# Attention and two MLPs on one core: each group of score and value matmuls ranked to run as one block on TensorE

## The chip, the cores and the metric

The kernel runs on one core of one Trainium2 chip. The metric is the device time of one execution in microseconds. Three runs of the kernel before took 1076.14 to 1080.6 us, with a median of 1076.39 us. The profile is of one execution, whose span from the first to the last instruction is 1075.8 us.

## The reference

Three layers follow each other. Shapes are those of the inputs.

```python
def _attn_ref(q, k, v, f):            # q, k, v: (4, 8, 576, 64), f: (4, 8, 576)
    scores = scale * np.matmul(q, k.transpose(0, 1, 3, 2))
    cum = np.cumsum(np.log(np.clip(f, 0.0001, 1.0)), axis=-1)
    scores = np.where(causal, -1000000000.0, scores + cum[:, :, :, None] - cum[:, :, None, :])
    attn = np.exp(scores - np.max(scores, axis=-1, keepdims=True))
    attn = attn / (np.sum(attn, axis=-1, keepdims=True) + 1e-09)
    return np.matmul(attn, v)
# x = attention's output as 2304 tokens of 512
# MLP 1: h = x @ w_in; r = max(h, 0); x = (s * r * r + b) @ w_out     (512 -> 2048 -> 512)
# MLP 2: h = x @ w_in; g = max(0.01 * h, h); out = g @ w_out          (512 -> 2048 -> 512)
```

## The kernel before

**Units.** The queries of each of the four batches are cut into a first unit (256 queries) and a second one (320 queries: two blocks of 128 and a tail of 64). A unit's eight heads are worked off in pairs. Attention on unit u+1 runs while MLP 1 works on unit u, so that TensorE (PE) gets two kinds of work in one stream. When attention is over, the rest of MLP 1 and then MLP 2 run alone.

**Attention's matmuls.** `mm_score` makes one score group for the two heads of a pair: for each query block two float32 matmuls with 64 rows, one for each head, on the lower and upper half of the partitions (L290), and then bfloat16 matmuls of an identity with a mask (L300). The 64 tail queries of both heads are one tile of two float32 matmuls with 128 rows (L279) and one mask matmul (L282). All go to one PSUM tile `ps_s`, of which there is one buffer. `st_score` reads it with VectorE (L320) and ScalarE takes the exponential (L338). `st_split` makes float16 high and low parts (L363 on ScalarE, L364 on VectorE) into `p_hl` (three buffers), and a transposing DMA on SyncE's queue brings them to `p_t` (L368, three buffers). `st_av` then issues the value products into `ps_v` (L385): float16, a weight load of 128 columns and a matmul each, with 128 columns for a block of queries and 64 for a tail. A tile of one head has 6 or 8 products, a tail 20 for the two heads; there are 104 such groups.

**The MLP's matmuls.** MLP 1 goes through 16 blocks of 128 hidden columns. `mlp1_h` issues 12 matmuls of 256 columns into `ps_h` (L696) and `mlp1_o` issues 12 of the block before into `ps_o` (L740; L737 in the first unit). Between them `mlp1_g` makes `g` out of `ps_h`: three passes on ScalarE (L718, L719, L720) and one on VectorE (L721). Operands are in the 4-byte format float32r, each value as a high and a low part, hence three products. MLP 2 has the same form in float32r with 512 columns (L798, L814).

**What sets the order.** The program is traced, and a scheduler with its own timeline of each engine then picks, for each engine, the next instruction among those that it holds ready; of several it takes the one with the highest rank. The rank follows the order of the source, shifted by `tc.high_priority(offset=n)`: `slots_to` traces each attention slot with a shift of 150 (scores, splits) or 90 (value products). The result is a fixed order for each engine, and semaphores for what crosses engines. On the chip each engine works its list in that order.

Of the kernel before, what the change touches and what calls it, by code (L numbers as in the profile page):

```python
# [1 line left out]

# [15 lines left out]
P = 128  # L18
UN = 256
# [19 lines left out]
def attention_moe_moe_kernel(  # L39
# [15 lines left out]
    nc = tc.nc  # L55
# [11 lines left out]
    NL = S - 2 * UN  # L67
# [80 lines left out]
    ident_h = const.tile([P, P], BF16, name="ident_h")  # L148
    mask_h = const.tile([P, P], BF16, name="mask_h")
    mask_l = const.tile([P, NL], BF16, name="mask_l")  # L150
# [35 lines left out]
    def q_cols(u):  # L186
        return UN + (2 * NL if units[u][2] > UN else 0)
# [6 lines left out]
    qk_p, cumk, v_raw, v_st, v_inv = {}, {}, {}, {}, {}  # L194
# [41 lines left out]
    def split_v(j, kend):  # L236
# [22 lines left out]
        for r in range(2):  # L259
# [3 lines left out]
                in_=hl[r * D : (r + 1) * D, :nk].rearrange("p k l c -> p (k l c)"),  # L263
            )

    def mm_score(i):

        jb, n, ts, last = tiles[i]
        u, h, j, half = jobs[jb]
        if not half and h % 2:  # L270
            return
        b, u0, un, _ = units[u]
        qk = qk_p[j // 2]
        qn = q_cols(u)
        ps = s_t[i] = ps_a.tile([P, 2, 512], F32, tag="ps_s", name="ps_s", bufs=1)
        if half:
            w = (u0 + un) // 2
            for c in range(2):
                nc.tensor.matmul(  # L279
                    ps[:, c, :w], qk[:, UN:qn], qk[:, qn + c * w : qn + (c + 1) * w], start=True, stop=c == 0  # L280
                )
            nc.tensor.matmul(ps[:, 1, w - NL : w], ident_h, mask_l, start=False, stop=True)  # L282
            return
        s_t[i + 1] = ps
        at = [sum(sum(QT[t]) for t in ts[:r]) for r in range(len(ts) + 1)]
        for r, t in enumerate(ts):
            q0, m = QT[t]
            for e in range(2):
                rows = slice(e * D, (e + 1) * D)
                nc.tensor.matmul(  # L290
                    ps[:, e, at[r] : at[r + 1]],
                    qk[rows, q0 - u0 : q0 - u0 + m],
                    qk[rows, qn : qn + q0 + m],
                    start=(r == 0),
                    stop=False,
                )

        for r, t in enumerate(ts):
            for e in range(2):
                nc.tensor.matmul(  # L300
                    ps[:, e, at[r + 1] - P : at[r + 1]], ident_h, mask_h, start=False, stop=(r == len(ts) - 1)
                )

    def st_score(i):
        jb, n, ts, last = tiles[i]
        u, h, j, half = jobs[jb]
        b, u0, un, _ = units[u]
        mm_score(i)
        ps = s_t.pop(i)
        tt = t_t[i] = ap.tile([P, S], F32, tag="tt", name="tt", bufs=4)  # L310
# [32 lines left out]
    def last_of_pair(jb):  # L343
        u, h, j, half = jobs[jb]
        return half or (h % 2 == 1 and units[u][2] == UN)
# [24 lines left out]
    def st_av(i):  # L370
        jb, n, ts, last = tiles[i]
        u, h, j, half = jobs[jb]
        b, u0, un, _ = units[u]
        if half or (n == 0 and h % 2 == 0):
            av_t[j // 2] = ps_a.tile([P, 512], F32, tag="ps_v", name="ps_v", bufs=2)
        av, pt = av_t[j // 2], p_t.pop(i)
        to = 0
        for t in ts:
            q0, m = QT[t]
            nk = -(-(q0 + m) // P)  # L380
            at = 0 if half else q0 - u0 + h % 2 * UN
            for e in range(P // m):
                for k in range(nk):
                    for l in range(2):
                        nc.tensor.matmul(  # L385
                            av[:, at + e * m : at + (e + 1) * m],
                            v_st[j + e][:, k].rearrange("p l d -> p (l d)"),
                            pt[:, to + l * nk + k, e * m : (e + 1) * m],
                            start=(k == 0 and l == 0),
                            stop=(k == nk - 1 and l == 1),  # L390
                        )
            to += 2 * nk
        if not last:
            return
        pr = h // 2
        if not half and h % 2 == 0:
            x_raw[u] = xp.tile([P, UN + NL], F32, tag="x_raw", name="x_raw", bufs=2)
        xr = x_raw[u]
        at = UN if half else 0
        for e in range(2) if half else [h % 2]:  # L400
            own, oth = slice(e * D, (e + 1) * D), slice((1 - e) * D, (2 - e) * D)
            m = NL if half else UN
            src, o = av[:, e * m : (e + 1) * m], xr[own, at : at + m]
            nc.scalar.copy(o, src[oth])
            nc.vector.tensor_tensor(out=o, in0=src[own], in1=o, op=ALU.add)
        if not last_of_pair(jb):
            return
        if pr == 0:
            xs[u] = xp.tile([P, 2, ND, UN], F32R, tag="x", name="x", bufs=2)
        inv = v_inv[j - j % 2][:, 4:5]  # L410
        with ahead(P_X):
            split_x1(xs[u], pr, xr[:, :UN], inv)
            if un > UN:
                xl = xr[:, UN:]
                nc.gpsimd.tensor_scalar(xl, xl, inv, 0.0, ALU.mult, ALU.add)
                nc.sync.dma_start(out=xld[pr * P : (pr + 1) * P, b * NL : (b + 1) * NL], in_=xl)

    def split_x1(x, d, raw, inv):
        nc.scalar.mul(x[:, 0, d], raw, inv)
        nc.vector.scalar_tensor_tensor(x[:, 1, d], raw, inv, x[:, 0, d].bitcast(F32), ALU.mult, ALU.subtract)  # L420
# [10 lines left out]
            )  # L431

    P_ATT, P_AV, P_G, P_W, P_F, P_X = 150, 90, 0, -100, 0, 100

    def ahead(n):
        return tc.high_priority(offset=n)
# [16 lines left out]
    def slot_d(i):  # L453
        if 0 <= i - LAG < NTL:
            st_av(i - LAG)
# [197 lines left out]
    c = 0  # L653
# [37 lines left out]
    def mlp1_h(u, i):  # L691
        x, (wi, wo) = xs[u], w1.get(i)
        ps = h_bank()[:, :UN]
        for d in range(ND):
            for n, (a, c) in enumerate(((0, 0), (0, 1), (1, 0))):
                nc.tensor.matmul(  # L696
                    ps,
                    wi[:, a, d * P : (d + 1) * P],
                    x[:, c, d],
                    start=(d == 0 and n == 0),  # L700
                    stop=(d == ND - 1 and n == 2),
                )
        return ps
# [128 lines left out]
    for u in range(NU):  # L832
# [9 lines left out]
        for i in range(NF):  # L842
# [12 lines left out]
            ps = mlp1_h(u, i)  # L855
# [99 lines left out]
```

## Time and profile before

| what | value |
|---|---|
| median of three runs | 1076.39 us (1076.14 to 1080.6) |
| profiled execution | span 1075.8 us, 18112 instructions |
| PE busy | 1036.2 us, 96% of the span |
| weight loads (PEld) busy | 877.7 us, 82% |
| VectorE, ScalarE, GpSimd busy | 544.3, 521.9 and 152.0 us |
| value products L385 | 912 matmuls, mean 216 ns each |
| score matmuls L290 | 224 records, mean 515 ns each |

A busy PE is not a PE at its peak: matmuls are pipelined, the end of one is modelled, and the mean durations above overlap. What an instruction costs the stream is the distance from its start to the start of the next, which the timeline shows. A float32 matmul (L290, L279) leaves two records in the trace, a float16, bfloat16 or float32r matmul one. The granted clock is 0.984 of full speed as a mean over the span.

### The profile page before, as it was taken

The numbers are of one execution on the slowest core, as the hardware profiler recorded it, in microseconds if no ns is written. First come the engines' busy times: TensorE is split into PE (matmuls) and PEld (weight loads), VectorE is DVE, ScalarE is ACT, GpSimd is POOL, SyncE is SP. The second block draws the span as 40 slices with busy tenths as digits, with TensorE's granted clock in tenths as the row PEclk, the third lists the DMA queues.
The fourth block names the chain that finished last, engine by engine and source line by source line (L and its number), as shares of the span: only waits on it lengthen the run. The fifth ranks groups of instructions, "written<-read, shape, count | busy, mean of one in ns | idle before, by whom it ended". The sixth has DMA issues, their size and how long they took to land.

```text
span 1075.8 us, 18112 instructions
## 1 busy us (share of the span) xinstructions
PE 1036.2 (96%) x6664; PEld 877.7 (82%) x6664; DVE 544.3 (51%) x1410; ACT 521.9 (49%) x1283; POOL 152.0 (14%) x234
## 2 busy tenths in 40 slices
PE   7888889999999999999999999999999999999998
PEld 4677779888787878878899999777888888888897
DVE  5899874665565765766633178983311311211111
ACT  4676786655565655655654366462222221222222
POOL 4334333010010000000000024451000000000000
PEclk9898889999999999999999999999999999999999
DMA  8499372666767866886822083640200100000010
GB/s 285 151 241 254 90 187 48 139 147 124 164 146 150 193 148 142 191 165 134 152 41 79 1 273 119 193 140 1 79 1 1 59 1 1 4 36 1 1 40 20
DMA packets 184296, 116.68 MB, mean 108 GB/s; under 512 B 137040, under 2 KB 163152, under 8 KB 184208
## 3 DMA queue, kind: packets, MB, share of 16 engines
q1 hardware_dynamic: 184208, 115.53, 43.9%
q8 instruction: 52, 0.85, 0.3%
q14 instruction: 36, 0.29, 0.1%
HBM read 74.00 MB, written 10.04 MB: 78 GB/s over the span
## 4 chain that ended last, share of the span: by engine, by line
PE 40%; issue 5%; DVE 3%; POOL 2%; DMA 1%; ACT 1%; SPq 0%; POOLq 0%; ACTq 0%; DVEq 0%
PE ps_o L814 16%; PE ps_h L798 15%; PE ps_o L740 4%; PE ps_h L696 3%; POOL w L111 2%; DVE wt L103 1%; DMA w_raw<-in_moe_w_out 1%; DVE wt L105 1%; DVE wt L102 1%; DMA p_t<-p_hl 0%; PE ps_v L385 0%; ACT wt L101 0%; PE ps_s L290 0%; DVE g L721 0%; DMA xld<-x_raw 0%
## 5 line engine op out<-in xcount | busy, mean ns | idle before, releaser
L696 PE MATMUL ps_h<-x,w 128*128 128x256 f32 x1728 | 275.4, 298 | 5.0 <-POOL w L111 3.3
L696 PEld LDWEIGHTS ps_h<-x,w 128*128 128x128 f32 x1728 | 238.5, 194 | 14.1 <-issue 6.5
L740 PE MATMUL ps_o<-g,w 128*128 128x256 f32 (+1 forms) x1536 | 245.8, 298 | 4.2 <-ACT g L720 1.5
L740 PEld LDWEIGHTS ps_o<-g,w 128*128 128x128 f32 x1536 | 209.8, 192 | 20.5 <-issue 7.6
L814 PE MATMUL ps_o<-w,g 128*128 128x512 f32 x864 | 216.1, 396 | 1.8 <-DVE g L806 1.8
L798 PE MATMUL ps_h<-x,w 128*128 128x512 f32 (+1 forms) x960 | 213.6, 370 | 0.0
L798 PEld LDWEIGHTS ps_h<-x,w 128*128 128x128 f32 x960 | 169.0, 188 | 34.3
L814 PEld LDWEIGHTS ps_o<-w,g 128*128 128x128 f32 x864 | 160.4, 188 | 41.6 <-DVE g L806 3.6
L806 DVE TENSOR_TENSOR g<-ps_h,g 128x512 fp32r<-128x512 f32 (+1 forms) x80 | 51.0, 637 | 258.3 <-ACT g L805 258.1
L804 ACT ACTIVATE ps_h<-ps_h 128x512 f32<-128x512 f32 (+1 forms) x80 | 43.1, 539 | 250.7 <-PE ps_h L798 250.7
L385 PE MATMUL ps_v<-p_t,v_st 128*128 128x128 f16 (+1 forms) x912 | 117.6, 216 | 10.1 <-DMA p_t<-p_hl 5.3
L364 DVE SCALAR_TENSOR_TENSOR p_hl<-tt,sm,p_hl 128x512 f16<-128x512 f32 (+4 forms) x128 | 80.8, 645 | 58.1 <-ACT p_hl L363 57.3
L363 ACT ACTIVATE p_hl<-tt,sm 128x512 f16<-128x512 f32 (+4 forms) x128 | 73.5, 597 | 54.7 <-DMA p_t<-p_hl 44.9
L718 ACT ACTIVATE ps_h<-ps_h 128x256 f32<-128x256 f32 x128 | 47.1, 368 | 92.0 <-PE ps_h L696 90.4
L111 POOL TENSOR_TENSOR w<-wt,w 128x512 fp32r<-128x512 f32 x48 | 73.9, 1542 | 98.5 <-ACT w L110 95.4
L385 PEld LDWEIGHTS <-v_st 128*128 128x128 f16 x912 | 62.7, 98 | 30.6 <-issue 9.1
L338 ACT ACTIVATE tt<-tt,sm 128x512 f32<-128x512 f32 (+4 forms) x128 | 76.2, 596 | 22.1 <-DVE sm L320 21.2
L721 DVE TENSOR_TENSOR g<-ps_h,g 128x256 fp32r<-128x256 f32 x128 | 53.7, 421 | 64.9 <-ACT g L720 63.8
L320 DVE CUSTOM_DVE_ANT_0 tt<-ps_s,cumk 128x512 f32<-128x512 f32 (+4 forms) x128 | 59.7, 498 | 18.4 <-PE ps_s L300 17.2
L290 PE MATMUL ps_s<-qk_p 64*128 64x512 f32 (+3 forms) x224 | 63.1, 515 | 2.1 <-issue 1.4
L101 ACT ACTIVATE wt<-w_raw 128x512 f32<-128x512 f32 x64 | 42.8, 673 | 30.7 <-POOL w L111 19.2
L720 ACT CAST g<-ps_h 128x256 fp32r<-128x256 f32 x128 | 47.0, 369 | 8.5 <-PE ps_o L740 5.3
(91 smaller groups left out, 877.1 us busy)
## 6 DMA issues: line engine op xcount, KB each, us to landing
w_raw<-in_moe_w_in SPq DMA_DIRECT2D x32, 512.0 KB, 6.0
w_raw<-in_moe_w_out SPq DMA_DIRECT2D x32, 512.0 KB, 6.2
cumk<-cumd SPq DMA_DIRECT2D x32, 256.0 KB, 3.9
qk_p<-in_qk SPq DMA_DIRECT2D x16, 480.0 KB, 4.2
x1d<-x1o SPq DMA_DIRECT2D x36, 128.0 KB, 2.8
cumk<-cumd SPq DMA_DIRECT2D x32, 144.0 KB, 3.2
v_raw<-in_v SPq DMA_DIRECT2D x16, 288.0 KB, 3.2
out<-o SPq DMA_DIRECT2D x18, 256.0 KB, 2.4
```

Of the source, the lines that this page charges most:

```text
L111: nc.gpsimd.tensor_tensor(w[:, 1], x, w[:, 0].bitcast(F32), ALU.subtract)
L290: nc.tensor.matmul(ps[:, e, at[r] : at[r + 1]], qk[rows, q0 - u0 : q0 - u0 + m], qk[rows, qn : qn + q0 + m], start=(r == 0), stop=False,)
L320: nc.vector.tensor_tensor_reduce(tt[:, at + k0 : at + k0 + kw], ps[:, c, :kw] if half else ps[:, h % 2, at : at + w], cumk[jb][:, k0 : k0 ...
L338: nc.scalar.activation(e, e, AF.Exp, bias=sm[:, r : r + 1], scale=-1.0, accum_out=sm[:, 2 + r : 3 + r])
L363: nc.scalar.mul(v[:, 0, :w], e, inv)
L364: nc.vector.scalar_tensor_tensor(v[:, 1, :w], e, inv, v[:, 0, :w], ALU.mult, ALU.subtract)
L385: nc.tensor.matmul(av[:, at + e * m : at + (e + 1) * m], v_st[j + e][:, k].rearrange("p l d -> p (l d)"), pt[:, to + l * nk + k, e * m : ( ...
L696: nc.tensor.matmul(ps, wi[:, a, d * P : (d + 1) * P], x[:, c, d], start=(d == 0 and n == 0), stop=(d == ND - 1 and n == 2),)
L721: nc.vector.tensor_tensor(out=g[:, 1, :UN], in0=ps, in1=g[:, 0, :UN].bitcast(F32), op=ALU.subtract)
L740: nc.tensor.matmul(po[d], wo[:, a, d * P : (d + 1) * P], g[:, c], start=(first and n == 0), stop=(last and n == 2),)
L798: nc.tensor.matmul(ps[:, :n], wi[:, a, d * P : (d + 1) * P], x[:, e, d, :n], start=(d == 0 and k == 0), stop=(d == ND - 1 and k == 2),)
L814: nc.tensor.matmul(po[m], g[:, a, m * P : (m + 1) * P], wo[:, e, :], start=(i == 0 and k == 0), stop=(i == NF - 1 and k == 2),)
```

## The change

A constant P_RUN of 4000 is added, and a helper `run_on(first)` that shifts the rank by it unless `first` is true. Of each score group, each tail's score group and each tile's group of value products, the first matmul keeps its rank and all others get the shift. Nothing else differs: every engine has the same instructions as before, in another order.

```diff
+    def run_on(first):
+        return nullcontext() if first else tc.high_priority(offset=P_RUN)
...
         if half:
             w = (u0 + un) // 2
             for c in range(2):
-                nc.tensor.matmul(
-                    ps[:, c, :w], qk[:, UN:qn], qk[:, qn + c * w : qn + (c + 1) * w], start=True, stop=c == 0
-                )
-            nc.tensor.matmul(ps[:, 1, w - NL : w], ident_h, mask_l, start=False, stop=True)
+                with run_on(c == 0):
+                    nc.tensor.matmul(
+                        ps[:, c, :w], qk[:, UN:qn], qk[:, qn + c * w : qn + (c + 1) * w], start=True, stop=c == 0
+                    )
+            with run_on(False):
+                nc.tensor.matmul(ps[:, 1, w - NL : w], ident_h, mask_l, start=False, stop=True)
             return
...
             for e in range(2):
                 rows = slice(e * D, (e + 1) * D)
-                nc.tensor.matmul(
...
+                with run_on(r == 0 and e == 0):
+                    nc.tensor.matmul(
...
                 for k in range(nk):
                     for l in range(2):
-                        nc.tensor.matmul(
...
+                        with run_on(t == ts[0] and e == k == l == 0):
+                            nc.tensor.matmul(
...
     P_ATT, P_AV, P_G, P_W, P_F, P_X = 150, 90, 0, -100, 0, 100
+    P_RUN = 4000
```

The line numbers of PE's matmuls move with the diff: L279 to L283, L282 to L287, L290 to L296, L300 to L307, L385 to L393, L696 to L705 and L740 to L749. The first place below is a score group of a second unit on PE's list (`ps_s_3725`). In the kernel before, with matmuls of MLP 1 (`ps_h_3260`) and single value products of the tail before it (`ps_v_3494`) between its two halves:

```order
L696 MATMUL ps_h_3260<-x_2323,w_383 128x256 x5
L385 LDWEIGHTS v_st_3044
L385 MATMUL ps_v_3494<-p_t_3436,v_st_3044 128x64
L696 MATMUL ps_h_3260<-x_2323,w_383 128x256
L290 MATMUL ps_s_3725<-qk_p_3397 128x512
L385 LDWEIGHTS v_st_3044
L385 MATMUL ps_v_3494<-p_t_3436,v_st_3044 128x64
L696 MATMUL ps_h_3260<-x_2323,w_383 128x256
L385 LDWEIGHTS v_st_3044
L385 MATMUL ps_v_3494<-p_t_3436,v_st_3044 128x64
L696 MATMUL ps_h_3260<-x_2323,w_383 128x256
L290 MATMUL ps_s_3725<-qk_p_3397 128x512
```

The same score group on PE's list of the changed kernel:

```order
L749 MATMUL ps_o_3175<-g_3071,w_1391 128x256 x6
L296 MATMUL ps_s_3725<-qk_p_3397 128x512 x2
L307 LDWEIGHTS ident_h_74
L307 MATMUL ps_s_3725<-mask_h_75,ident_h_74 128x128
L307 LDWEIGHTS ident_h_74
L307 MATMUL ps_s_3725<-mask_h_75,ident_h_74 128x128
L393 LDWEIGHTS v_st_3338
L393 MATMUL ps_v_3564<-p_t_3562,v_st_3338 128x128
```

The two halves and the two masks of the group now stand next to each other, and the products of the tail before it stand, all twenty together, further ahead on the list.

The second place is a group of eight value products (`ps_v_3564` out of `p_t_3492`) on PE. In the kernel before, where they alternate with the output matmuls of MLP 1 (`ps_o`):

```order
L740 MATMUL ps_o_3175<-g_3202,w_1397 128x256 x4
L385 LDWEIGHTS v_st_3336
L385 MATMUL ps_v_3564<-p_t_3492,v_st_3336 128x128
L740 MATMUL ps_o_3176<-g_3202,w_1397 128x256
L385 LDWEIGHTS v_st_3336
L385 MATMUL ps_v_3564<-p_t_3492,v_st_3336 128x128
L740 MATMUL ps_o_3176<-g_3202,w_1397 128x256
```

The start of the same group in the changed kernel:

```order
L705 MATMUL ps_h_3189<-x_2323,w_308 128x256 x12
L393 LDWEIGHTS v_st_3336
L393 MATMUL ps_v_3564<-p_t_3492,v_st_3336 128x128
L393 LDWEIGHTS v_st_3336
L393 MATMUL ps_v_3564<-p_t_3492,v_st_3336 128x128
```

Six more such pairs follow there before the next matmul of MLP 1, so the group of eight is one run behind a whole block of twelve.

## Rows read from the trace of the kernel before

**Rows 1.** The page: span, and PE's busy time.

```profile
span 1075.8 us, 18112 instructions
PE 1036.2 (96%) x6664; PEld 877.7 (82%) x6664; DVE 544.3 (51%) x1410; ACT 521.9 (49%) x1283; POOL 152.0 (14%) x234
```

**Rows 2.** Stretches: length, busy us (count) of PE, PEld, DVE, ACT, POOL, PEclk, DMA.

```profile
200.00:250.00 50.00, 45.50 (x387) 40.76 (x386) 30.14 (x90) 29.56 (x76) 5.81 (x14) 1.00 0.68 143
...
200.00:560.00 360.00, 354.80 (x2843) 297.10 (x2841) 222.33 (x672) 214.67 (x553) 28.52 (x81) 1.00 0.72 148
```

**Rows 3.** Timeline of PE (start, duration, instruction): a whole MLP block, then a wait.

```profile
224.50 1.56 PE L696 MATMUL ps_h<-x,w 128*128 128x256 f32 x12
225.90 0.90 PE L385 MATMUL ps_v<-p_t,v_st 128*128 128x128 f16 x13
227.74 0.50 PE L740 MATMUL ps_o<-g,w 128*128 128x256 f32 x2 [0.93 <-ACT g L720]
```

**Rows 4.** Timeline of PE: products of 128 columns in alternation.

```profile
401.24 0.23 PE L385 MATMUL ps_v<-p_t,v_st 128*128 128x128 f16 x1
401.27 0.36 PE L740 MATMUL ps_o<-g,w 128*128 128x256 f32 x1
...
402.70 0.23 PE L385 MATMUL ps_v<-p_t,v_st 128*128 128x128 f16 x1
```

**Rows 5.** Timeline of PE: six products in a run, then a split score pair.

```profile
427.31 0.51 PE L385 MATMUL ps_v<-p_t,v_st 128*128 128x128 f16 x6
427.63 0.95 PE L696 MATMUL ps_h<-x,w 128*128 128x256 f32 x6
428.52 0.91 PE L290 MATMUL ps_s<-qk_p 64*128 64x384 f32 x2
429.36 0.39 PE L696 MATMUL ps_h<-x,w 128*128 128x256 f32 x1
429.67 0.91 PE L290 MATMUL ps_s<-qk_p 64*128 64x384 f32 x2
430.51 0.38 PE L696 MATMUL ps_h<-x,w 128*128 128x256 f32 x1
430.74 0.23 PE L300 MATMUL ps_s<-mask_h,ident_h 128*128 128x128 bf16 x1
```

**Rows 6.** Timeline of PE: a tail's products, first in alternation, then in a run.

```profile
416.47 0.20 PE L385 MATMUL ps_v<-p_t,v_st 128*128 128x64 f16 x1
...
417.70 0.20 PE L385 MATMUL ps_v<-p_t,v_st 128*128 128x64 f16 x1
...
435.19 0.48 PE L385 MATMUL ps_v<-p_t,v_st 128*128 128x64 f16 x11
435.51 2.38 PE L740 MATMUL ps_o<-g,w 128*128 128x256 f32 x18
437.73 1.12 PE L696 MATMUL ps_h<-x,w 128*128 128x256 f32 x8
```

**Rows 7.** Timeline of PE: a score pair of 384 columns together.

```profile
408.38 0.92 PE L290 MATMUL ps_s<-qk_p 64*128 64x384 f32 x4
409.23 0.28 PE L300 MATMUL ps_s<-mask_h,ident_h 128*128 128x128 bf16 x2
```

**Rows 8.** Timeline of PE: score pairs of 512 columns, together and split.

```profile
234.38 1.13 PE L290 MATMUL ps_s<-qk_p 64*128 64x512 f32 x4
235.44 0.28 PE L300 MATMUL ps_s<-mask_h,ident_h 128*128 128x128 bf16 x2
...
418.69 1.12 PE L290 MATMUL ps_s<-qk_p 64*128 64x512 f32 x2
419.75 0.39 PE L740 MATMUL ps_o<-g,w 128*128 128x256 f32 x1
```

**Rows 9.** Who waited for tile p_t (us, times), and its DMA's time to landing.

```profile
  ACT p_hl L363: 44.9, 30
...
DMA to landing us min/median/max: 2.7/3.4/6.6
```

More of the change, by code (lines that the diff above doesn't have):

```diff
@@ L1 @@
-from contextlib import ExitStack
+from contextlib import ExitStack, nullcontext
 import concourse.bass as bass
@@ L289, in mm_score @@
                 rows = slice(e * D, (e + 1) * D)
-                nc.tensor.matmul(
[L291 to L296, printed above, removed]
+                with run_on(r == 0 and e == 0):
+                    nc.tensor.matmul(
+                        ps[:, e, at[r] : at[r + 1]],
+                        qk[rows, q0 - u0 : q0 - u0 + m],
+                        qk[rows, qn : qn + q0 + m],
+                        start=(r == 0),
+                        stop=False,
+                    )
         for r, t in enumerate(ts):
             for e in range(2):
-                nc.tensor.matmul(
-                    ps[:, e, at[r + 1] - P : at[r + 1]], ident_h, mask_h, start=False, stop=(r == len(ts) - 1)
-                )
+                with run_on(False):
+                    nc.tensor.matmul(
+                        ps[:, e, at[r + 1] - P : at[r + 1]], ident_h, mask_h, start=False, stop=(r == len(ts) - 1)
+                    )
     def st_score(i):
@@ L384, in st_av @@
                     for l in range(2):
[L385 to L391, printed above, removed]
+                        with run_on(t == ts[0] and e == k == l == 0):
+                            nc.tensor.matmul(
+                                av[:, at + e * m : at + (e + 1) * m],
+                                v_st[j + e][:, k].rearrange("p l d -> p (l d)"),
+                                pt[:, to + l * nk + k, e * m : (e + 1) * m],
+                                start=(k == 0 and l == 0),
+                                stop=(k == nk - 1 and l == 1),
+                            )
             to += 2 * nk
```

## The prediction

> **What bounds the kernel now.** I read the page's busy times first: PE is busy for 1036.2 of 1075.8 us, and no other engine for more than half of the span [rows 1]. The table of stretches says where: from 200 to 560 us, while attention and MLP 1 share PE, PE is busy for 354.8 of 360 us at the full granted clock (1.00, the 2.4 GHz level), VectorE for 222.3 and ScalarE for 214.7 [rows 2]. Of the 5.2 us in which PE is idle there, 4.5 lie in the first 50 us. So in this stretch time is what PE's stream takes, and what makes the stream shorter makes the kernel shorter, until something else comes late.
>
> Busy does not say that PE works at its pace, so I read the timeline, from start to start. Twelve MLP matmuls in a row take 1.40 us, 0.117 each [rows 3]. Six value products in alternation with six MLP matmuls go from 401.24 to 402.70, 1.46 us, 0.243 for a pair [rows 4]; the products themselves are short, for a run of six takes 0.32 us, 0.053 each [rows 5]. Alternating thus costs more than its parts: 0.243 against 0.117 + 0.053. The same holds for the tails' products of 64 columns: five pairs take 1.23 us, 0.246 each, and a run of eleven takes 0.32 us, 0.029 each [rows 6].
>
> **The change part by part.** Every engine has the instructions that it had. What changes is the order, and only from the 385th of the 3190 rows of PE's list on. I counted PE's list, taking matmuls of one kind in a row as a run: 1503 runs before, 757 now.
>
> *Boundaries.* A product, or a mask matmul, that is followed by an MLP matmul occurs 461 times before (235 products of 128 columns, 162 of 64, 64 masks) and 133 times now (68, 16 and 49). To price one, I put a run beside an alternation. After a run, eighteen MLP matmuls take 435.51 to 437.73, 2.22 us [rows 6]; less seventeen at 0.118 that leaves 0.21 for the first of them, where the others take 0.118: the surcharge falls once for each run, on the matmul behind it, and a little on the run's own start. Six products in a run with six MLP matmuls behind cost 0.32 + 0.21 + 5 x 0.118 = 1.12 us, in alternation 1.46. The 0.34 lie on five boundaries: 0.068 each. For the tails: 6 x 0.029 + 0.02 for the start + 0.80 = 0.99 against 6 x 0.246 = 1.48, so 0.098 each. The masks I price like the products of 128 columns.
> 167 x 0.068 = 11.4; 146 x 0.098 = 14.3; 15 x 0.068 = 1.0. Together 26.7 us.
>
> The Trainium skill (TensorE: Matmul & The Clock Gate, "Back-to-back issue gap") puts a sustained stream of weight loads and matmuls at about 81 ns each for 128 columns, not at the 0.053 us of the row. By that each of the 167 products that join a run would take 0.028 us longer, 4.7 us in all, and the saving would be 42 instead of 47 us. The run of six here is at odds with it, and I go by the run.
>
> *Score pairs.* The two heads' score matmuls sit on different halves of the rows. Where they stand together, four records of 384 columns take 408.38 to 409.23, 0.85 us [rows 7], and one half alone takes just as long, 428.52 to 429.36, 0.84 [rows 5]: the second half is free when it stands next to the first. For 512 columns it is 1.06 together and 1.06 for a half alone [rows 8]. On PE's list 17 pairs are split now (9 of 384 columns, 7 of 512, 1 of 128), and none after the change: 9 x 0.84 + 7 x 1.06 + 0.3 = 15.3 us. The 0.3 is an estimate, 128/384 of the 0.84.
>
> *MLP matmuls beside scores.* One between two halves takes 0.31 (429.36 to 429.67), one behind the second half 0.23 (430.51 to 430.74) [rows 5], against 0.118. So being behind a score costs 0.11 and being before one the other 0.08. The list has 30 of the first kind before and none now, 41 and 33 of the second: 30 x 0.11 + 8 x 0.08 = 3.9 us.
>
> *Tails' score matmuls.* They are not a pair that can share, both use 128 rows. 11 MLP matmuls behind one go, for 0 to 11 x 0.11 = 1.2 us. I take 0.8.
>
> Sum of the stream: 26.7 + 15.3 + 3.9 + 0.8 = 46.7 us.
>
> *New waits.* The other engines now have some 47 us less for the same attention work. ScalarE would be busy for 214.7 of about 313 us instead of 360, 69% instead of 60%, and VectorE 71%: neither becomes the bound by its sum. But both work in order, and one place shows how PE gets caught: at 227.74 PE waits 0.93 us for g from L720, behind a block of twelve, a run of thirteen products and nothing else [rows 3], and ScalarE in turn sat 44.9 us in all, 30 times, in front of L363 until a p_t transpose had read its p_hl buffer [rows 9]. A moved group takes with it who waits for it: the p_t buffer that its last product frees starts the next transpose on SyncE's queue, that frees p_hl, that lets ScalarE go on to the MLP's g. In runs, the last product of a group comes earlier than its alternating form would, which helps, while the time between groups shrinks. Both ends: no new wait at all (0), or the idle share of the stretch 200 to 250, where the groups already stand in runs for the most part, 4.5 in 50 us [rows 2], over the some 265 us that the rest of the shared stretch would take: 24 us. The nearest row is the whole shared stretch, 5.2 us of idle time [rows 2]; I take as much again, 5 us.
>
> The profile's span is 0.6 us under the median of the runs. 1075.8 - 46.7 + 5 = 1034.1 for the span, and 1034.7 with the 0.6: **1035 us**.
>
> **Rivals.**
>
> 1. *The waits take the place.* PE, 12% faster, finds g, ps_s or p_t late all along, as at 227.74. For it: ps_s has a single buffer, p_t lands 3.4 us after its issue and up to 6.6 [rows 9], and these don't get shorter. Against it: from 250 to 560 us PE is idle for 0.7 us in all [rows 2], so what PE needs lies ready today. Price: idle time of 10 to 24 us, so 1040 to 1054; with as much as 30, 1060. The Trainium skill names the pattern for faster matmuls (TensorEngine Tiling, "PSUM Bottleneck"): reading PSUM out may become the bottleneck after them.
>
> 2. *Slower, through the transposes.* Each of the 104 groups is now one indivisible run. If PE reaches a group's first product before its p_t has landed, the MLP matmuls that used to fill in stand behind on the list, and PE sits. If all 104 waited like 227.74, that is 97 us: 1076 - 47 + 97 = 1126. The rival decides from 47/104 = 0.45 us a group. For it: the 3.4 us landing and the 44.9 us of ScalarE [rows 9]. Against it: the runs of the stretch 200 to 250 cost 4.5 us in all [rows 2].
>
> 3. *Starts that don't mean time.* The distances could be the profile's modelling, or the surcharge be paid for something that every matmul has to wait for anyway (a weight load, 82% busy [rows 1]); then about nothing changes: 1071 to 1081. Against it: start-to-start distances add up to the stretch, and the rows for splits need no model at all.
>
> 4. *More than counted.* The stream alone, without new waits, gives 1076.4 - 46.7 = 1030; if the 4.5 us of idle time from 200 to 250 go as well, 1025; with a surcharge a tenth larger, 1021. So 1020 to 1027. For it: earlier ends of groups free buffers earlier. Against it: nothing in the rows shows a wait that the boundaries cause.
>
> **How the numbers follow.** Forecast (1027 to 1043, waits of 0 to 13 us) 0.62; rival 1 (above 1043) 0.20; rival 4 0.08; rival 3 0.05; rival 2 0.05. The range for 8 in 10 goes from 1025 to 1054: it takes in the stream alone without waits (1030), a surcharge that is mis-sized by a tenth, and the 24 us of waits. About 0.5%, 5.4 us, is what a measurement here can tell from no change. Faster by more than that are the forecast, rivals 1 and 4: 0.90; the same, rival 3: 0.05; slower, rival 2: 0.05.
>
> **What would show it.** In the changed kernel's timeline, products in runs at 0.053 and 0.029 us each with one MLP matmul of about 0.21 behind; score pairs of 0.85 and 1.06 us, never a half alone; attention's last value product some 40 us earlier, and everything after it shifted with its own length unchanged. PE's idle time after 200 us should be about 10 us; 25 or more would be rival 1, with g from L720 and p_t as the releasers. The forecast is wrong if the runs are there but their matmuls keep the distances of the alternation.

## The result, and the profile after

The changed kernel took 1039.38 us (median of four runs, 1039.15 to 1045.3), against 1078.28 us for the kernel before in the same comparison (median of four, 1076.14 to 1080.6). The ratio is 0.9654, with a 95% interval of 0.963 to 0.9678: 3.5% faster. The forecast was 1035 us in a range of 1025 to 1054.

The page of the changed kernel answers to [rows 1]; columns are an engine, its busy time and share, and its count.

```profile
span 1037.7 us, 18127 instructions
PE 986.1 (95%) x6664; PEld 851.0 (82%) x6664; DVE 537.9 (52%) x1410; ACT 521.3 (50%) x1283; POOL 151.8 (15%) x234
```

PE has as many records as before and is busy for 50.1 us less, while the span is shorter by only 38.1. The stretches show where. Of the kernel before, cut at the point up to which both lists of PE are the same, and at the start of the last value product:

```profile
0.00:141.90 141.90, 117.58 (x683) 97.48 (x683) 116.55 (x337) 95.77 (x266) 55.14 (x68) 0.89 0.74 205
141.90:560.60 418.70, 411.07 (x3297) 348.71 (x3295) 256.22 (x793) 254.89 (x669) 46.98 (x101) 1.00 0.68 142
560.60:1075.80 515.20, 507.57 (x2688) 431.55 (x2687) 171.50 (x281) 171.25 (x350) 49.86 (x65) 1.00 0.17 55
```

And of the changed kernel, cut at the same two points (the columns are those of [rows 2]):

```profile
0.00:138.40 138.40, 110.93 (x683) 91.09 (x684) 114.72 (x333) 93.56 (x258) 55.44 (x68) 0.95 0.76 205
138.40:517.60 379.20, 361.97 (x3249) 322.49 (x3247) 250.16 (x795) 254.54 (x671) 46.15 (x101) 1.00 0.80 158
517.60:1037.70 520.10, 513.24 (x2742) 437.43 (x2738) 173.06 (x283) 173.17 (x355) 50.25 (x65) 1.00 0.16 54
```

- The first stretch holds the same 683 PE records in the same order, and is still 3.5 us shorter. Its granted clock is 0.95 instead of 0.89: PE is busy for 6.6 us less and idle for 3.1 us more. PE's list there is not touched by the change, so the 3.5 us are not counted as its work.
- In the shared stretch PE's busy time falls by 49.1 us and its idle time rises from 7.6 (418.70 - 411.07) to 17.2 us (379.20 - 361.97).
- The last stretch is 4.9 us longer, since the list has 54 more records behind the last value product (2742 against 2688). Attention now ends earlier in MLP 1's work.

Busy time that the change took from PE's stream: 50.1 in all less the 6.6 of the first stretch, so 43.4 us. Idle time that it brought: 9.6 us in the shared stretch.

The timeline of the changed kernel shows one tile's work, with start, duration and instruction; it answers to [rows 4 to 7].

```profile
348.76 1.57 PE L705 MATMUL ps_h<-x,w 128*128 128x256 f32 x12
350.18 0.51 PE L393 MATMUL ps_v<-p_t,v_st 128*128 128x128 f16 x6
350.62 0.92 PE L296 MATMUL ps_s<-qk_p 64*128 64x384 f32 x4
351.46 0.28 PE L307 MATMUL ps_s<-mask_h,ident_h 128*128 128x128 bf16 x2
351.56 1.66 PE L749 MATMUL ps_o<-g,w 128*128 128x256 f32 x12
353.06 1.60 PE L705 MATMUL ps_h<-x,w 128*128 128x256 f32 x12
354.50 0.76 PE L393 MATMUL ps_v<-p_t,v_st 128*128 128x64 f16 x20
355.10 1.30 PE L749 MATMUL ps_o<-g,w 128*128 128x256 f32 x6
356.24 0.51 PE L393 MATMUL ps_v<-p_t,v_st 128*128 128x128 f16 x6
356.56 0.96 PE L749 MATMUL ps_o<-g,w 128*128 128x256 f32 x6
```

Read the starts: twenty products of a tail take 354.50 to 355.10, 0.030 each (0.246 in alternation, [rows 6]), six of 128 columns 0.32 in front of MLP matmuls (356.24 to 356.56) and 0.44 in front of a score pair (350.18 to 350.62), and the score pair 350.62 to 351.46, 0.84 us for both halves. Twelve output matmuls behind a group take 351.56 to 353.06, 1.50 us, against 1.42 for the twelve between 348.76 and 350.18: one surcharge of 0.08 for the whole run.

PE's waits from 200 to 520 us of the changed kernel (who waited for whom, us, times, longest) show the other side:

```profile
PE ps_o L749 <- ACT g L729: 6.3, 6, 1.5
PE ps_v L393 <- DMA p_t<-p_hl: 4.1, 6, 1.0
```

### The profile page after: what moved, and what is told of

It reads as the page before. It is cut to its first block, busy times and chain, and to the rows that moved or that the text cites. A ratio compares the mean times of both kernels' runs of the same rounds, so it can differ in the third digit from the quotient of the medians.

```text
span 1037.7 us, 18127 instructions
## 1 busy us (share of the span) xinstructions
PE 986.1 (95%) x6664; PEld 851.0 (82%) x6664; DVE 537.9 (52%) x1410; ACT 521.3 (50%) x1283; POOL 151.8 (15%) x234
## 4 chain that ended last, share of the span: by engine, by line
PE 47%; issue 3%; DVE 3%; POOL 2%; DMA 1%; ACT 1%; POOLq 0%; SPq 0%; ACTq 0%; DVEq 0%
PE ps_o L823 17%; PE ps_h L807 16%; PE ps_o L749 6%; PE ps_h L705 6%; POOL w L111 2%; PE ps_v L393 1%; DVE wt L103 1%; DMA w_raw<-in_moe_w_out 1%; DVE wt L105 1%; DVE wt L102 1%; PE ps_s L296 1%; DMA p_t<-p_hl 0%; ACT wt L101 0%; PE ps_s L283 0%; DVE g L730 0%
## 5 line engine op out<-in xcount | busy, mean ns | idle before, releaser
L705 PE MATMUL ps_h<-x,w 128*128 128x256 f32 x1728 | 242.9, 286 | 5.0 <-POOL w L111 3.3
L749 PE MATMUL ps_o<-g,w 128*128 128x256 f32 (+1 forms) x1536 | 226.8, 289 | 10.8 <-ACT g L729 6.3
L705 PEld LDWEIGHTS ps_h<-x,w 128*128 128x128 f32 x1728 | 220.4, 190 | 7.7 <-POOL w L111 3.9
L749 PEld LDWEIGHTS ps_o<-g,w 128*128 128x128 f32 x1536 | 197.3, 190 | 17.5 <-ACT g L729 7.9
L807 PEld LDWEIGHTS ps_h<-x,w 128*128 128x128 f32 x960 | 169.0, 188 | 34.4
L371 DVE SCALAR_TENSOR_TENSOR p_hl<-tt,sm,p_hl 128x512 f16<-128x512 f32 (+4 forms) x128 | 77.5, 619 | 34.3 <-ACT p_hl L370 33.8
L370 ACT ACTIVATE p_hl<-tt,sm 128x512 f16<-128x512 f32 (+4 forms) x128 | 73.2, 595 | 40.2 <-DMA p_t<-p_hl 31.6
L393 PE MATMUL ps_v<-p_t,v_st 128*128 128x128 f16 (+1 forms) x912 | 59.7, 211 | 14.7 <-DMA p_t<-p_hl 11.9
L727 ACT ACTIVATE ps_h<-ps_h 128x256 f32<-128x256 f32 x128 | 46.8, 367 | 50.3 <-PE ps_h L705 49.4
L393 PEld LDWEIGHTS <-v_st 128*128 128x128 f16 x912 | 44.3, 98 | 21.4 <-issue 13.2
L101 ACT ACTIVATE wt<-w_raw 128x512 f32<-128x512 f32 x64 | 42.7, 672 | 28.2 <-POOL w L111 19.8
L729 ACT CAST g<-ps_h 128x256 fp32r<-128x256 f32 x128 | 47.2, 370 | 7.9 <-PE ps_o L749 4.4
L728 ACT ACTIVATE ps_h<-ps_h 128x256 f32<-128x256 f32 x128 | 46.9, 368 | 3.0
```

Source lines behind the costliest of these rows:

```text
L370: nc.scalar.mul(v[:, 0, :w], e, inv)
L371: nc.vector.scalar_tensor_tensor(v[:, 1, :w], e, inv, v[:, 0, :w], ALU.mult, ALU.subtract)
L393: nc.tensor.matmul(av[:, at + e * m : at + (e + 1) * m], v_st[j + e][:, k].rearrange("p l d -> p (l d)"), pt[:, to + l * nk + k, e * m : ( ...
L705: nc.tensor.matmul(ps, wi[:, a, d * P : (d + 1) * P], x[:, c, d], start=(d == 0 and n == 0), stop=(d == ND - 1 and n == 2),)
L749: nc.tensor.matmul(po[d], wo[:, a, d * P : (d + 1) * P], g[:, c], start=(first and n == 0), stop=(last and n == 2),)
L807: nc.tensor.matmul(ps[:, :n], wi[:, a, d * P : (d + 1) * P], x[:, e, d, :n], start=(d == 0 and k == 0), stop=(d == ND - 1 and k == 2),)
```

## The experiments

Each was timed against the kernel before on the same chip, in three batches: first products alone, scores alone, four `p_hl` buffers and g first; then the three kernels with added matmuls and the first run with four `p_t` buffers; then the four of the last table. The kernel before had a median of 1078.1 to 1078.7 us in all of them.

**Products alone, scores alone.** In the first, all `run_on` of `mm_score` is off, in the second that of `st_av`:

```diff
-                with run_on(r == 0 and e == 0):          # products alone; the other three of mm_score likewise
+                with run_on(True):
...
-                        with run_on(t == ts[0] and e == k == l == 0):   # scores alone
+                        with run_on(True):
```

Products alone, as expected:

> Only the value products get the high rank, scores and masks keep theirs. On PE's list 151 products or masks are followed by an MLP matmul (461 before, 133 with the whole change) and 11 score pairs stay split (8 of 384 columns, 2 of 512, 1 of 128). Theory A (each boundary and each split pair costs PE what the timeline showed, and PE's stream sets the time): against the whole change the stream is longer by 8 x 0.84 + 2 x 1.06 + 0.3 = 9.1 us for the split pairs, 45 MLP matmuls behind a score x 0.11 = 5.0, and 18 boundaries x 0.068 = 1.2, together 15 us: some 1054 us with the same waits, 1046 if all the new waits go. Theory B (the gain comes from the score groups, which bring the next tile's data earlier; product boundaries are only a modelling of the trace): near 1070.

Scores alone, as expected:

> Only the scores and masks get the high rank, the value products keep theirs. No score pair is split, and 418 boundaries remain (227 behind products of 128 columns, 137 of 64, 54 masks). Theory A: against the whole change the stream is longer by 159 x 0.068 + 121 x 0.098 + 5 x 0.068 = 23 us, less the new waits that a slower PE would not meet (up to 9): 1053 to 1062 us. Theory B: near the whole change, 1040 to 1045.

Measured: 1054.80 us, ratio 0.9784 (0.9757 to 0.9812), for the products alone, and 1058.22 us, 0.981 (0.9791 to 0.9829), for the scores alone. Both lie where the sum over boundaries and split pairs puts them, and far from what theory B gave for either. The totals depend on which run of the whole change they are held against (1039.38, or 1044.35 below), so PE's own time is the better test. The stretch from PE's 683rd record to the last value product, with products alone and then with scores alone:

```profile
141.00:536.40 395.40, 376.83 (x3247) 329.76 (x3246) 249.83 (x791) 252.75 (x665) 47.91 (x101) 0.99 0.78 150
140.40:538.90 398.50, 387.77 (x3295) 338.82 (x3293) 252.29 (x794) 254.36 (x670) 47.44 (x101) 1.00 0.74 150
```

With products alone PE is busy for 14.9 us more than the 361.97 of the whole change, where the count gave 15. With scores alone it is 25.8 us more here and 5.2 less behind, since 46 of the MLP's matmuls have moved into the stretch: 20.6, where the count gave 23. In the timeline of the products alone a pair is still split, and still paid twice:

```profile
340.80 0.91 PE L296 MATMUL ps_s<-qk_p 64*128 64x384 f32 x2
341.64 0.39 PE L705 MATMUL ps_h<-x,w 128*128 128x256 f32 x1
341.96 0.91 PE L296 MATMUL ps_s<-qk_p 64*128 64x384 f32 x2
342.80 0.38 PE L705 MATMUL ps_h<-x,w 128*128 128x256 f32 x1
```

The two halves take 340.80 to 341.64 and 341.96 to 342.80, 0.84 us each. With scores alone the products still alternate; two successive starts of products in its timeline are 0.24 us apart:

```profile
331.49 0.23 PE L393 MATMUL ps_v<-p_t,v_st 128*128 128x128 f16 x1
331.53 0.36 PE L705 MATMUL ps_h<-x,w 128*128 128x256 f32 x1
331.73 0.23 PE L393 MATMUL ps_v<-p_t,v_st 128*128 128x128 f16 x1
```

The two gains (23 and 20 us) add up to more than the whole, 39 us. The counts point the same way: with the scores in runs the products have fewer boundaries too (418 instead of 461), and with the products in runs fewer pairs are split (11 instead of 17). By the sums the overlap is some 9 us of stream; the idle time of PE in the stretch (18.6 us with products alone, 10.7 with scores alone, 17.2 with both, 7.6 before) takes about half of that out of the totals.

**The price of a boundary by itself.** Three kernels add 176 matmuls to the last unit of MLP 1, where no attention is left. Their moving operand is zero, so `ps_h` keeps its value.

```diff
+                if u == NU - 1 and (d < ND - 1 or n < 2):     # run: (d == 0 and n == 0)
+                    for _ in range(1):                        # run: range(11)
+                        nc.tensor.matmul(ps[:, :P], ident_h, zero_h[:, :P], start=False, stop=False)   # wide: UN for P
```

Alternating, 128 columns, as expected:

> The whole change, and in the last unit of MLP 1, where no attention is left, 176 additional bfloat16 matmuls of 128 columns that add zero to ps_h, one behind each MLP matmul but the last of a block of twelve. Theory A (a boundary costs 0.068 us beside the 0.053 of the matmul): 176 x 0.121 = 21 us more than the whole change, about 1060 us, and the timeline shows pairs of 0.243. If a boundary costs nothing (the distances are modelled): 176 x 0.053 = 9 us, 1049.

In runs of eleven, as expected:

> The same 176 additional matmuls of 128 columns that add zero, but eleven in a row behind the first MLP matmul of each block. Theory A: 176 x 0.053 + 16 x 0.068 = 10.4 us more than the whole change, about 1050 us, that is 11 us less than in alternation. If only the number of matmuls counts: the same as in alternation.

Alternating, 256 columns, as expected:

> As the alternation of 176 matmuls that add zero, with 256 columns instead of 128. Two explanations of the surcharge: (1) the MLP matmul's weight load (0.19 to 0.20 us in the trace) starts when the matmul ahead of it starts, and what is not covered by that matmul's stream is paid: 256 columns cover as much as an MLP matmul does, so a pair takes about 2 x 0.119 us and the 176 cost 176 x 0.119 = 21 us, about 1060 us, the same as the half as wide ones. (2) The surcharge is the price of the change between operand formats, however wide the matmul: 176 x (0.107 + 0.068) = 31 us, 1070.

Measured: 1068.13 us alternating, 1055.43 in runs, and 1066.66 with 256 columns. In runs it is 12.7 us less than in alternation for the same matmuls (11 expected). Against the 1039.38 of the whole change all three are 5 to 8 us longer than expected. In their own stage they are not: the same 400 MLP matmuls or so take 51.6 us in the whole change (579.7 to 631.3 us), 72.8 alternating, 64.7 in runs and 74.5 with 256 columns. By their counts of PE records these stretches hold 172, 165 and 171 of the 176 added matmuls; the first few stand ahead of them. The stretches, of the four kernels in this order, one fence for each:

```profile
579.70:631.30 51.60, 50.73 (x402) 48.94 (x401) 39.51 (x65) 31.98 (x76) 17.04 (x13) 1.00 0.60 205
```

```profile
588.00:660.80 72.80, 71.85 (x574) 63.91 (x573) 52.91 (x84) 38.93 (x87) 28.73 (x19) 1.00 0.58 189
```

```profile
585.40:650.10 64.70, 62.27 (x567) 58.82 (x566) 50.10 (x76) 36.25 (x84) 25.89 (x16) 1.00 0.61 196
```

```profile
587.60:662.10 74.50, 72.64 (x573) 64.20 (x573) 54.05 (x84) 39.49 (x88) 29.85 (x19) 1.00 0.57 184
```

Alternation costs 21.2 us there, 0.123 for each of 172, where the price was 0.121. The runs cost 13.1 us for 165 of them, where 10.4 had been expected for all: PE is idle for 1.6 us more (64.70 - 62.27 against 51.60 - 50.73), and the scheduler cut twelve of the sixteen runs into pieces, 34 runs in all. The other 5 to 8 us lie in earlier stretches, where the scatter between executions of one kernel is of this size (1039 to 1045 in the result); what part of them is the added constant's doing stays open. The wide ones tell the two explanations apart: their pairs are 0.24 us apart as well, though each streams twice the columns. In its timeline (start, duration, instruction):

```profile
600.73 0.28 PE L716 MATMUL ps_h<-zero_h,ident_h 128*128 128x256 bf16 x1
600.76 0.36 PE L707 MATMUL ps_h<-x,w 128*128 128x256 f32 x1
600.97 0.28 PE L716 MATMUL ps_h<-zero_h,ident_h 128*128 128x256 bf16 x1
```

So the surcharge is not a fixed price of changing the operand format, which would have put the pairs at 0.29 us. It behaves like the first explanation, by which a short matmul leaves open what a wide one covers: at 64, 128 and 256 columns alike a pair takes about what two MLP matmuls take (2 x 0.118 us). That it is the MLP matmul's weight load which is paid for is not shown: no run changed the load alone. Nor was a run of 256 columns by itself timed; the 0.107 us is twice the 0.053.

**The new waits.** Two kernels give the changed one a fourth buffer, of `p_hl` or of `p_t`, and one ranks the MLP's passes to `g` before attention.

```diff
-        ph = ap.tile([P, 10 * P], F16, tag="p_hl", name="p_hl", bufs=3)     # or both tiles of tag p_t, 3 to 4
+        ph = ap.tile([P, 10 * P], F16, tag="p_hl", name="p_hl", bufs=4)
...
-    P_ATT, P_AV, P_G, P_W, P_F, P_X = 150, 90, 0, -100, 0, 100              # g first
+    P_ATT, P_AV, P_G, P_W, P_F, P_X = 150, 90, 300, -100, 0, 100
```

Four p_hl buffers, as expected:

> The whole change with four p_hl buffers instead of three (there is no room for a fourth of both). Theory A says that the whole change lost about 10 us to new waits, behind ScalarE's passes of the MLP and p_t's transposes. If ScalarE's wait for a free p_hl buffer (31.6 us, 19 times, in front of L370) is what holds the MLP's g back, PE's waits for g from L729 (6.3 us after 200 us) fall below 2 us and the time by 4 to 6: 1034 to 1036. If p_t lands late whatever ScalarE does (DMA queues busy for 0.9 to 1.0 of the time from 300 to 500 us), the time stays within 2 us of 1039.

The MLP's g first, as expected:

> The whole change, and the MLP's passes from ps_h to g ranked before the attention's work (shift of 300 instead of 0). If PE's new waits are a matter of the order on ScalarE, the 6.3 us of waits for g go and 1033 to 1036 us are left. If they are a matter of work that ScalarE can't start (it sits in front of a pass that waits for a transpose), the order changes little: 1037 to 1041. If attention's chain then comes late, PE waits for p_t instead and the time rises above 1042.

Four p_t buffers, as expected:

> The whole change with four p_t buffers instead of three. SyncE's queue waited 21 us in front of L375 for PE to free a p_t buffer. If that is the start of the chain behind PE's new waits (p_t late, then p_hl, then g), the waits for p_t (4.1 us after 200 us) and for g (6.3) shrink by half or more and the time falls to 1033 to 1036. If the transposes are late since the DMA queues are full, it stays within 2 us of 1039.

Measured: 1037.53 us with four p_hl buffers (ratio 0.9617, 0.9596 to 0.9638), 1036.86 with four p_t buffers (0.9618, 0.9583 to 0.9654), and 1063.98 with g first (0.9855, 0.9823 to 0.9888). The two buffers were under the whole change by less than their intervals tell apart; with four p_hl buffers PE's waits for g from L729 did fall, from 6.3 to 2.9 us (140 to 520 us), not quite below the 2 that was expected. Ranking g first loses most of the gain, as its third branch said: PE's waits for p_t rise to 12.4 us from 140 to 540 us (4.1 in the whole change), and g from L729 is as late as before, 6.3 us. Its top waits:

```profile
PE ps_v L393 <- DMA p_t<-p_hl: 12.4, 9, 2.4
PE ps_o L749 <- ACT g L729: 6.3, 5, 3.2
```

These waits are a part of the loss only. PE's list there has 131 boundaries and no split pair, counted in the trace, so its stream is no longer by the count. Of the 25.5 us by which its profiled span is longer than the whole change's, 15.0 lie in the stretch from PE's 683rd record to the last value product. There PE is idle for 27.8 us instead of 17.2, and busy for 4.4 us more, at a granted clock of 0.98 instead of 1.00:

```profile
146.20:540.40 394.20, 366.42 (x3246) 327.99 (x3245) 248.71 (x792) 254.12 (x671) 46.65 (x101) 0.98 0.76 152
```

Another 7.8 us lie ahead of that, where its list differs from the whole change's as well, and what they come from stays open.

To tell few us apart, four kernels were then run in more rounds on one chip: the whole change, four p_t buffers, four buffers of both (the room comes from `x1o`, one buffer instead of two), and the kernel before with four p_t buffers.

```diff
-            o = mp.tile([P, UN], F32, tag="x1o", name="x1o", bufs=2)        # both buffers
+            o = mp.tile([P, UN], F32, tag="x1o", name="x1o", bufs=1)
```

The whole change again, as expected:

> The whole change once more, on the same chip as the three that follow, so that a difference of few us can be told: 1039 us.

Four p_t buffers again, as expected:

> The whole change with four p_t buffers, now beside the whole change itself. PE's list has the same stream (133 boundaries, no split pair). If the fourth buffer takes away part of the new waits, as its first profile shows (3.4 us of idle time on PE from the 1200th to the 2466th MLP matmul instead of 7.6), it is 3 to 5 us under the whole change; if the first run was scatter, within 1.5 us of it.

Four buffers of both, as expected:

> The whole change with four p_t and four p_hl buffers; the room comes from one x1o buffer instead of two (MLP 1's output on its way to memory, four times a unit). If both buffers act on the same chain, no more than with four p_t buffers: 1034 to 1037. If they add, 1031 to 1034. What the single x1o buffer costs, at the 9 unit ends, is bounded by 9 x 3 us of a store's landing, though most of it is beside PE's work.

The kernel before with four p_t buffers, as expected:

> The kernel before, without the high rank, with four p_t buffers. Theory A counts its list alone: 536 boundaries instead of 461 (267 behind products of 128 columns, 211 of 64, 58 masks) and 19 split pairs instead of 17 (two more of 512 columns). That makes 32 x 0.068 + 49 x 0.098 - 6 x 0.068 + 2 x 1.06 + 5 x 0.11 = 9 us more stream, so it is slower than the kernel before by 6 to 9 us, near 1086, although a buffer was added. If buffers help whatever the order, or if boundaries cost nothing, it is at or under the kernel before.

Measured:

| kernel | median us | ratio to the kernel before, 95% interval |
|---|---|---|
| whole change | 1044.35 | 0.968 (0.9662 to 0.9697) |
| whole change, four p_t buffers | 1037.19 | 0.9618 (0.9601 to 0.9636) |
| whole change, four of both, one x1o | 1058.69 | 0.9814 (0.9798 to 0.9831) |
| kernel before, four p_t buffers | 1086.69 | 1.0073 (1.006 to 1.0086) |

The whole change missed its expected 1039 by 5 us. In the first run one execution of four was as slow (1045.3 us); here all were (1042.03 to 1046.18). Its profile (span 1043.5 us, 5.8 more than in the first run) has the same counts on PE's list, 133 boundaries and no split pair; 4.2 of the 5.8 us are idle time of PE. The stretch from PE's 683rd record to the last value product:

```profile
139.00:523.40 384.40, 362.98 (x3247) 322.47 (x3246) 249.64 (x792) 254.37 (x671) 45.65 (x101) 1.00 0.78 156
```

PE is busy for 363.0 us there (362.0 in the first run) and idle for 21.4 (17.2). Why the waits differ between two runs of one kernel is not shown.

The fourth p_t buffer makes the changed kernel faster beside it, by 7.2 us where 3 to 5 were expected, with intervals that don't touch; against the first run of the whole change (0.963 to 0.9678) the intervals overlap a little. The four p_hl buffers, run once, are level with it (0.9617). From 280 to 520 us PE is busy for 237.09 us with it, and in the whole change for 230.19. The stretch of the whole change, then that with four p_t buffers:

```profile
280.00:520.00 240.00, 230.19 (x2103) 202.00 (x2104) 166.08 (x523) 161.96 (x419) 20.33 (x61) 1.00 0.90 172
```

```profile
280.00:520.00 240.00, 237.09 (x2190) 210.74 (x2188) 169.78 (x533) 166.80 (x432) 21.05 (x60) 1.00 0.88 174
```

PE's waits for g from L729 from 140 to 520 us fall from 8.1 to 4.9 us by it, and those for p_t from 5.8 to 0.6 us. Two fences, the whole change and four p_t buffers:

```profile
PE ps_o L749 <- ACT g L729: 8.1, 7, 2.5
PE ps_v L393 <- DMA p_t<-p_hl: 5.8, 6, 1.6
```

```profile
PE ps_o L749 <- ACT g L729: 4.9, 7, 1.4
PE ps_v L393 <- DMA p_t<-p_hl: 0.6, 1, 0.6
```

So a part of the new waits starts at the p_t buffers, and the DMA queues, at 0.88 to 0.90 of the time in both, do not forbid a gain. Both buffers with one x1o were expected at 1031 to 1037 and took 1058.69: PE waits 8.0 us for p_t and 4.7 for VectorE's reading of ps_s there. It is not the count of the list, which by its trace has 122 boundaries and no split pair. PE is idle for 28.2 us from its 683rd record to the last value product, and busy for 5.1 us more than in the whole change, at a granted clock of 0.98:

```profile
141.90:537.20 395.30, 367.07 (x3247) 327.05 (x3246) 247.81 (x788) 251.57 (x664) 46.00 (x102) 0.98 0.75 151
```

Whether the single x1o buffer or another order of the engines' work brings these waits was not separated.

The kernel before with a fourth p_t buffer is slower, by 8.0 us, where the count of its list gave 9. From PE's 683rd record to the last value product PE is busy for 419.8 us instead of 411.1, 8.7 more:

```profile
140.70:570.80 430.10, 419.82 (x3298) 352.99 (x3297) 256.86 (x794) 254.90 (x671) 45.75 (x101) 1.00 0.66 139
```

The count of boundaries and split pairs foretold that a kernel gets slower by one more buffer; that buffers help in any order, the other view, did not hold.

## Why the prediction was right

**The bound.** PE's stream set the time of the shared stretch. The 49.1 us of busy time that went there came off the span but for the 9.6 us of new idle time and the 4.9 us that moved behind attention; that leaves 34.6, and the 3.5 us of the first stretch make it 38.1.

**Boundaries and split pairs.** The sum was 46.7 us of stream; 43.4 were measured. Its two large terms held up one by one: an alternating matmul cost 0.123 us where the price gave 0.121, and PE's busy time in the two halves of the change and in the kernel before with another buffer came out within 3 us of their counts. The 3 us between sum and measurement are not placed; the price was made from a few rows, and a tenth of it was inside the range.

**Products in a run.** A run of six takes 0.32 us in the changed kernel, 356.24 to 356.56 above. By the 81 ns of the Trainium skill (TensorE: Matmul & The Clock Gate, "Back-to-back issue gap") it would take an estimated 0.49 us, and this trace does not agree.

**New waits.** This was the term that was mis-sized: 9.6 us of idle time in the shared stretch against 5, and 13.8 in the second run of the whole change (21.4 - 7.6), both inside the bounds of 0 to 24. For the waits for g the mechanism was the one named. PE waits for g, and ScalarE's timeline just ahead of the longest such wait, at 317.17 us in the changed kernel, shows the pass into p_hl (L370) held by a transpose, and the MLP's three passes (L727 to L729) queued behind it:

```profile
315.32 0.72 ACT L370 ACTIVATE p_hl<-tt,sm 128x512 f16<-128x512 f32 x1 [2.07 <-DMA p_t<-p_hl]
315.95 0.36 ACT L727 ACTIVATE ps_h<-ps_h 128x256 f32<-128x256 f32 x1
316.35 0.37 ACT L728 ACTIVATE ps_h<-ps_h 128x256 f32<-128x256 f32 x1
316.75 0.37 ACT L729 CAST g<-ps_h 128x256 fp32r<-128x256 f32 x1
```

PE's side of it, in the timeline of PE:

```profile
317.17 0.50 PE L749 MATMUL ps_o<-g,w 128*128 128x256 f32 x2 [1.51 <-ACT g L729]
```

That is [rows 3] once more, 1.51 us instead of 0.93. DMA's queues are busy for 0.80 of the shared stretch instead of 0.68, and a transpose lands after a median of 3.9 us instead of the 3.4 of [rows 9].

```profile
DMA to landing us min/median/max: 2.7/3.9/6.6
```

**The time.** 1034.1 was forecast for the span and 1037.7 measured. The stream gave 3.3 us less than its sum, the waits took 4.6 more than their term, and the first stretch gave 3.5 that no term had; the other 0.8 us are idle time that the last stretch lost. Without the 3.5 us, which the change doesn't explain, the span would have been 1041: that the forecast came so near is in part luck. Run a second time, the whole change took 1044.35 us, inside the range but above the 1043 at which the prediction drew the line between its forecast and rival 1. The last value product starts at 517.6 us instead of 560.6, 43 us earlier where some 40 were named. What stands behind it was foretold to keep its length; it is 4.9 us longer, for the 54 records that moved there.

**The rivals.** Rival 1, the waits in the place of the boundaries, is there in part: from 200 us to the last value product PE is idle for 13.6 us, and for 17.8 in the second run, where the forecast was about 10 and the rival 25. The releasers are the named ones, g and p_t; for VectorE's reading of ps_s PE waited 1.0 us. Rival 2 would have needed 0.45 us a group; the two kinds of wait above are 10.4 us over 104 groups, 0.1 each. Rival 3, distances that mean no time, fell with the alternation of 176. Rival 4 is not seen: the idle time grew.

## What to carry to other kernels

Where two kinds of matmul share TensorE, read the distance from start to start and not the busy share: 98% busy here held 43 us that only the order cost. In this kernel short matmuls belonged together in one run, and the two heads' matmuls on different rows next to each other; count the boundaries on the engine's list before changing anything else, since a changed buffer count can add some. What then comes late is the chain that the slower stream had hidden, so try one more buffer where that chain starts before giving the late engine another order.

## What the runs showed that was not expected

A bfloat16 matmul of 256 columns between two MLP matmuls costs hardly more than one of 128: pairs are 0.24 us apart in either case, and the stage is 1.7 us longer, 0.9 of it idle. Ranking the MLP's passes first, which looked harmless, gave back 25 of the 39 us. And the first stretch differs between executions although PE's list is the same up to where the lists part: 141.9 us at a granted clock of 0.89 in the kernel before, 138.4 at 0.95 in the changed one, and 139.0 at 0.91 in its second run, so its length does not follow the clock alone.
